# Query tiles of 128, 128, 128, 96 and 96 rows in a decay attention with a routed expert

## The chip, the cores and the metric

One core of a Trainium2 chip runs the whole program. The metric is device time in microseconds (us) of one execution. Engines are named as in the profile: PE multiplies, PEld loads PE's weights beside it, DVE, ACT and POOL do elementwise work, and SP, ACT and POOL issue transfers.

## What is computed

There are 8 batches of 8 heads, 576 tokens and 64 features in a head. Attention is causal, with a bias that decays with a running sum, and is followed by an expert that treats 128 chosen tokens of each batch.

```
scores = scale * q @ k.T;  cum = cumsum(max(s, 0))
scores = where(causal, -1e9, scores + min(-(cum_i - cum_j), 0))
attn = softmax(scores);  x = attn @ v          # heads side by side, 512 wide
score = x @ w_gate;  top = the 128 best tokens of each batch
out = x;  out[top] += sigmoid(score[top]) * (relu(x[top] @ w1) @ w2)
```

## The kernel before

576 tokens are cut into 5 tiles: four of 128 rows and a last one of 64 (`NT = 5`, `LAST = 64`). A head goes through these stages, each an entry of a hand-written list (`SCHEDULE`) that gives a stage its place in a period of 8 slots. Every engine runs its instructions in the order in which the program issues them, since all calls go through `InOrder`, whose line, L34, is the one that the profile shows.

- `s_part` (4 parts): scores with queries on the partitions, only for the row maximum. PE writes `s`, DVE reads it with the mask (`mj`) and leaves the maximum `m`. `m_rows` turns `m` on PE and sends it by ACT and a transfer into row `RM` of `QA`.
- `st_part` (L381, 4 parts): scores again, transposed, with key tile `t` on the partitions and the queries from that tile on along the columns, in two products each (`ka` by `qa`, `kb` by `qb`). Part 0 takes key tiles 1 (448 columns) and 4 (64 keys by 64 queries), part 1 tiles 2 and 3, parts 2 and 3 the two halves of tile 0. ACT takes the exponential into `pt`, and POOL clears the triangle of each tile's own block.
- `av` (L418): for query tile `u`, the sum over key tiles `t <= u` of `pt[t, u]` times `v`; `pt` is the weight operand, so its columns are the query rows. The operands are full-precision f32, and each product runs as two passes. Stage `av0` has tiles 0 and 1, `av1` tile 2, `av2` tile 3, `av3` tile 4. Full tiles take 95 columns of `vt`, the last tile 65 (`VO`, `VC`).
- `norm` (L436): DVE divides by the row sums, and after each 4 heads SP writes the block to `out`, in one transfer for the four full tiles and one for the last.
- `choose` (L482) and `expert` run between these stages in small steps, with `choose` mostly on DVE and `expert` on PE.

Buffers of `s`, `st` and `sct` share 4 PSUM banks (`psS`), so PE can be at most four of them ahead of their readers.

Of the kernel before, what the change touches and what calls it, by code (L numbers as in the profile page):

```python
# [7 lines left out]
F32 = mybir.dt.float32  # L8
F32R = mybir.dt.float32r
# [3 lines left out]
AF = mybir.ActivationFunctionType  # L13
# [6 lines left out]
def _f(ap):  # L20
    return ap.bitcast(F32)
# [45 lines left out]
def kernel(  # L67
# [32 lines left out]
    EPACE, CPACE = CFG["epace"], CFG["cpace"]  # L100


    cols = [S - P * t for t in range(NT)]
    order = [1, 4, 2, 3, 0]
    off = {}
    o = 0
    for t in order:
# [18 lines left out]


    NB = 4
    ka_all = const.tile([P, NB, S], F32R, tag="ka", name="ka")
    kb_all = const.tile([P, NB, S], F32R, tag="kb", name="kb")  # L130
    qa_all = const.tile([P, NB, SP], F32R, tag="qa", name="qa")
    qb_all = const.tile([P, NB, SP], F32R, tag="qb", name="qb")
    KA, KB, QA, QB = ([x[:, i, :] for i in range(NB)] for x in (ka_all, kb_all, qa_all, qb_all))
    warm = const.tile([P, 512], BF16, tag="warm", name="warm")
    dve.memset(warm, 0.0)
    zrow = moe.tile([2 * NH, S], F32, tag="row", name="zrow")
# [36 lines left out]
    act.activation(  # L173
        qa_all[D:RT, 1:NB], warm[D:RT, 0 : NB - 1].rearrange("p (a o) -> p a o", o=1).broadcast_to([RT - D, NB - 1, SP]), AF.Copy, bias=1.0
    )
    pool.memset(_f(ka_all[D:RT, 1:NB]), 1.0)
    maskf, ident = masks()
    pool.memset(_f(qa_all[0:D, :, 0:PAD]), 0.0)

# [28 lines left out]
    def choice_constants():  # L208

        pool.memset(earlier, 1.0)  # L210
        own = earlier[:, (NT - 1) * P : NT * P]
        pool.affine_select(
            out=own, in_=own, pattern=[[-1, P]], compare_op=ALU.is_ge,
            fill=0.0, base=-1, channel_multiplier=1,
        )
        pool.memset(later, 1.0)
        pool.affine_select(
            out=later[:, 0:P], in_=later[:, 0:P], pattern=[[1, P]], compare_op=ALU.is_ge,
            fill=0.0, base=0, channel_multiplier=-1,
        )  # L220
        place_i = moe.tile([P, S], I32, tag="hh", name="place_i")
        pool.iota(place_i, pattern=[[1, S]], base=0, channel_multiplier=0)
        token_i = const.tile([P, NT], I32, tag="token_i", name="token_i")
        pool.iota(token_i, pattern=[[P, NT]], base=0, channel_multiplier=1)
        dve.tensor_copy(place, place_i)
        dve.tensor_copy(token, token_i)
        wgrow = w_gate.rearrange("(o d) -> o d", o=1)
        sp.dma_start(wg, wgrow.broadcast_to([P, DM]))
# [33 lines left out]
    for i in range(2):  # L262
        bank = psA.tile([P, 512], F32, tag=f"av{i}", name=f"pa{i}")
        pa = bank[:, 0 : NT * EW].rearrange("p (t e) -> p t e", e=EW)
        dve.memset(pa[LAST:P, NT - 1, :], 1.0)
        PA.append(pa)


# [112 lines left out]
    def st_part(n, part):  # L381
        i = n % NB
        R = RM[i] + 1
        ka, kb, qa, qb = KA[i], KB[i], QA[i], QB[i]
        if part == 0:
            st[n]["pt"] = ptp.tile([P, PTW], F32, tag="pt", name=f"pt{n}")
        pt = st[n]["pt"]
        tp = psS.tile([P, 512], F32, tag="s", name=f"st{n}_{part}")
        plan = [
            [(1, 0, cols[1]), (4, 0, cols[4])],  # L390
            [(2, 0, cols[2]), (3, 0, cols[3])],
            [(0, 0, HALF)],
            [(0, HALF, HALF)],
        ][part]
        o = 0
        for t, c0, w in plan:
            kr = min(P, S - t * P)
            ks = slice(t * P, t * P + kr)
            qs = slice(PAD + t * P + c0, PAD + t * P + c0 + w)
            pe.matmul(tp[0:kr, o : o + w], ka[0:R, ks], qa[0:R, qs], start=True, stop=False)  # L400
            pe.matmul(tp[0:kr, o : o + w], kb[:, ks], qb[:, qs], start=False, stop=True)
            o += w
        p0 = off[plan[0][0]] + plan[0][1]
        if part == 0:
            act.activation(pt[:, p0 : p0 + cols[1]], tp[:, 0 : cols[1]], AF.Exp, scale=SCALE)
            act.activation(pt[0:LAST, p0 + cols[1] : p0 + o], tp[0:LAST, cols[1] : o], AF.Exp, scale=SCALE)
        else:
            act.activation(pt[:, p0 : p0 + o], tp[:, 0:o], AF.Exp, scale=SCALE)
        for t, c0, _ in plan:
            if c0 == 0:  # L410
                w = min(P, cols[t])
                pool.affine_select(
                    out=pt[0:w, off[t] : off[t] + w], in_=pt[0:w, off[t] : off[t] + w],
                    pattern=[[1, w]], compare_op=ALU.is_ge, fill=0.0, base=0,
                    channel_multiplier=-1,
                )

    def av(n, us):  # L418
        b, h = divmod(n, H)
        pt, vt, pa = st[n]["pt"], vts[n // 2], PA[n % 2]  # L420
        if us[0] == 0:
            if h == 0:
                xts[b] = xp.tile([P, NT, DM], F32, tag="xt", name=f"xt{b}")
        xt = xts[b]
        for u in us:
            w = P if u < NT - 1 else LAST
            for t in range(u + 1):
                kr = P if t < NT - 1 else LAST
                c0 = off[t] + (u - t) * P
                vo, vc, vw = (0, VC[n % 2], EW) if w == P else (VO[n % 2], (n % 2) * E1, E1)  # L430
                pe.matmul(
                    pa[0:w, u, vo : vo + vw], pt[0:kr, c0 : c0 + w], vt[0:kr, t, vc : vc + vw],
                    start=(t == 0), stop=(t == u),
                )

    def norm(n, part):  # L436
        b, h = divmod(n, H)
        xt = xts[b]
        if part == 0:
            st[n]["z"] = small.tile([P, NT], F32, tag="z", name=f"z{n}")  # L440
        z, pa, vo = st[n]["z"], PA[n % 2], VO[n % 2]
        if part == 0:
            dve.tensor_scalar(z, pa[:, :, vo + D], 1e-9, None, op0=ALU.add)
        elif part == 1:
            dve.reciprocal(z, z)
        else:
            dve.tensor_tensor(
                xt[:, :, h * D : (h + 1) * D], pa[:, :, vo : vo + D],
                z.rearrange("p (t o) -> p t o", o=1).broadcast_to([P, NT, D]),
                op=ALU.mult,  # L450
            )
        if part < 2:
            return
        if h % XH == XH - 1:
            es = slice((h + 1 - XH) * D, (h + 1) * D)
            sp.dma_start(
                out[b, 0 : (NT - 1) * P, es].rearrange("(t p) d -> p t d", p=P), xt[:, 0 : NT - 1, es]
            )
            sp.dma_start(out[b, (NT - 1) * P : S, es], xt[0:LAST, NT - 1, es])


    out_rows = out.rearrange("b s d -> (b s) d")
# [19 lines left out]
    def choose(b):  # L482
# [8 lines left out]
                yield CPACE[0]  # L491
        yield CPACE[0]

        row = moe.tile([P, NT * P], F32, tag="row", name=f"row{b}")
        for u0, u1 in ((0, 3), (3, NT)):
            tps = psS.tile([P, 512], F32, tag="s", name=f"sct{b}_{u0}")
            for t in range(u0, u1):
                pe.transpose(
                    tps[:, (t - u0) * P : (t - u0 + 1) * P], sc[:, t : t + 1].broadcast_to([P, P]), ident
                )  # L500
            act.activation(row[:, u0 * P : u1 * P], tps[:, 0 : (u1 - u0) * P], AF.Copy)
            if not finishing:
                yield CPACE[1]
        if finishing:
# [1 line left out]

        ahead = small.tile([P, 2, NT], F32, tag="ahead", name=f"ahead{b}")
        for t in range(NT):
            r = min(P, S - t * P)
            sj = sc[0:r, t : t + 1]  # L510
            for i, (c0, c1, mask, op) in enumerate((
                (0, t * P + r, earlier[0:r, (NT - 1 - t) * P : (NT - 1) * P + r], ALU.is_ge),
                (t * P, S, later[0:r, 0 : S - t * P], ALU.is_gt),
            )):
                junk = moe.tile([P, S], BF16, tag="junk", bufs=2, name=f"ahead{b}_{t}_{i}")
                dve.scalar_tensor_tensor(
                    junk[0:r, 0 : c1 - c0], row[0:r, c0:c1], sj, mask, op0=op, op1=ALU.mult,
                    accum_out=ahead[0:r, i, t : t + 1],
                )
                if not finishing:  # L520
                    yield CPACE[2]

        hits = []
        for si, (s0, n) in enumerate(slots):
            for t in range(NT):
                r = min(P, S - t * P)
                hit = moe.tile([P, P], F16, tag="hit", name=f"hit{b}_{si}_{t}", bufs=NT * len(slots))
                (pool if finishing and t in CFG["hp"] else dve).tensor_scalar(
                    hit[0:r, 0:n], place[0:r, s0 : s0 + n], ahead[0:r, 0, t : t + 1],
                    ahead[0:r, 1, t : t + 1], op0=ALU.subtract, op1=ALU.is_equal,  # L530
                )
                hits.append((hit, si, n, t, r))
                if not finishing:
                    yield CPACE[3]
# [288 lines left out]
```

## Time and profile before

| | us |
|---|---|
| median of 3 runs (lowest, highest) | 543.26 (538.83, 587.77) |
| the profiled execution | 537.0 |
| its span, first to last instruction | 535.2 |
| PE busy in it | 510.6 |
| DVE busy in it | 403.1 |
| POOL busy in it | 324.0 |
| ACT busy in it | 296.6 |

Busy shares are means over stages with different limits, and a PE that is busy is not a PE at its peak: its records overlap. The starts of successive weight loads show better how fast PE gets on.

### The profile page before, as it was taken

The numbers are of one execution on the slowest core, as the hardware profiler recorded it, in microseconds if no ns is written. First come the engines' busy times: TensorE is split into PE (matmuls) and PEld (weight loads), VectorE is DVE, ScalarE is ACT, GpSimd is POOL, SyncE is SP. The second block draws the span as 40 slices with busy tenths as digits, with TensorE's granted clock in tenths as the row PEclk, the third lists the DMA queues.
The fourth block names the chain that finished last, engine by engine and source line by source line (L and its number), as shares of the span: only waits on it lengthen the run. The fifth ranks groups of instructions, "written<-read, shape, count | busy, mean of one in ns | idle before, by whom it ended". The sixth has DMA issues, their size and how long they took to land.

```text
span 535.2 us, 11357 instructions
## 1 busy us (share of the span) xinstructions
PE 510.6 (95%) x3845; PEld 455.7 (85%) x3847; DVE 403.1 (75%) x1416; ACT 296.6 (55%) x658; POOL 324.0 (61%) x492
## 2 busy tenths in 40 slices
PE   6999998999989999999999999999999999999996
PEld 3788988889878888899888999998988898988774
DVE  7668896998899868867768886875689887763642
ACT  5557775657666747555444665544566665532121
POOL 7767775768787767755455774545578764523130
PEclk7999997999999979899999999999999999999999
DMA  4324541243425313323113332033242431011110
GB/s 160 106 97 133 170 142 44 72 141 115 150 75 152 117 59 123 104 89 94 46 69 116 111 114 71 3 116 110 74 132 65 140 95 41 9 46 40 65 39 21
DMA packets 23900, 49.08 MB, mean 92 GB/s; under 512 B 2538, under 2 KB 12069, under 8 KB 23843
## 3 DMA queue, kind: packets, MB, share of 16 engines
q1 hardware_dynamic: 19376, 39.52, 23.2%
q10 hardware_dynamic: 3186, 4.65, 2.8%
q0 software_dynamic: 1280, 4.20, 2.3%
q8 instruction: 30, 0.49, 0.4%
q14 instruction: 28, 0.22, 0.1%
HBM read 36.37 MB, written 11.53 MB: 90 GB/s over the span
## 4 chain that ended last, share of the span: by engine, by line
PE 65%; DVE 23%; issue 6%; DMA 2%; POOL 1%; ACT 1%; POOLq 0%; SPq 0%; DVEq 0%; ACTq 0%
PE pa L34 25%; PE st L34 15%; PE s L34 9%; DVE mj L34 8%; PE py L34 6%; DVE ahead L34 4%; DVE junk L34 3%; DVE qb L34 3%; PE warm L34 2%; DVE xt L34 1%; PE sct L34 1%; POOL hit L34 1%; DMA xe<-out_dram,idx 1%; DVE z L34 1%; DMA out_dram<-xt 1%
## 5 line engine op out<-in xcount | busy, mean ns | idle before, releaser
L34 PE MATMUL pa<-vt,pt 128*128 128x95 f32 (+2 forms) x1920 | 234.1, 261 | 0.0
L34 PEld LDWEIGHTS pa<-vt,pt 128*128 128x128 f32 (+2 forms) x1920 | 215.0, 176 | 18.4 <-issue 10.6
L34 DVE CUSTOM_DVE_ANT_0 mj<-s,maskf 128x192 bf16<-128x192 f32 (+4 forms) x320 | 140.7, 470 | 58.1 <-PE s L34 56.8
L34 ACT ACTIVATE pt<-st 128x288 f32<-128x288 f32 (+3 forms) x320 | 120.3, 430 | 106.4 <-PE st L34 87.6
L34 POOL TENSOR_SCALAR_AFFINE_SELECT pt<-pt 128x128 f32<-128x128 f32 (+1 forms) x320 | 96.1, 321 | 123.6 <-ACT pt L34 111.2
L34 PE MATMUL st<-qa,ka 67*128 67x288 f32 (+9 forms) x384 | 120.2, 330 | 13.5 <-DVE m L34 9.4
L34 POOL TENSOR_TENSOR qb<-qk,qb 64x576 fp32r<-64x576 f32 x62 | 95.7, 1544 | 31.6 <-DVE qb L34 22.1
L34 PE MATMUL s<-ka,qa 66*128 66x64 f32 (+4 forms) x384 | 110.7, 346 | 2.9 <-DVE ka L34 2.9
L34 POOL TENSOR_TENSOR kb<-qk,ka 64x576 fp32r<-64x576 f32 x64 | 95.2, 1488 | 8.2 <-ACT ka L34 3.1
L34 PE MATMUL st<-qb,kb 128*128 128x288 f32 (+4 forms) x384 | 100.1, 298 | 0.0
L34 PEld LDWEIGHTS st<-qa,ka 67*128 67x128 f32 (+3 forms) x384 | 70.6, 184 | 19.4 <-DVE m L34 11.3
L34 PEld LDWEIGHTS st<-qb,kb 128*128 128x128 f32 (+1 forms) x384 | 70.8, 184 | 4.8
L34 PEld LDWEIGHTS s<-ka,qa 66*128 66x128 f32 x384 | 65.4, 194 | 9.6 <-POOL qa L34 3.3
L34 ACT ACTIVATE kb<-qk 64x576 fp32r<-64x576 f32 x64 | 43.6, 683 | 5.4 <-DVE qb L34 1.2
L34 DVE CAST qb<-qk 64x576 fp32r<-64x576 f32 x64 | 44.3, 692 | 2.2 <-issue 0.2
L34 ACT ACTIVATE qa<-qk 64x576 fp32r<-64x576 f32 x64 | 43.7, 683 | 3.4 <-DMA qa<-mr 1.5
L34 ACT ACTIVATE ka<-qk 64x576 fp32r<-64x576 f32 x64 | 42.9, 670 | 4.1 <-DVE m L34 3.6
L34 ACT ACTIVATE mr<-s 5x128 fp32r<-5x128 f32 x63 | 16.8, 266 | 47.8 <-PE s L34 47.4
L34 DVE CUSTOM_DVE_ANT_0 junk<-xt,wg 128x512 bf16<-128x512 f32 (+1 forms) x40 | 37.4, 954 | 0.4
L34 DVE TENSOR_TENSOR xt<-pa,z 128x320 f32<-128x320 f32 x64 | 31.1, 486 | 0.1
L34 DVE SCALAR_TENSOR_TENSOR ahead<-row,sc,later 128x576 bf16<-128x576 f32 (+4 forms) x35 | 29.4, 840 | 0.6
L34 POOL DMA_INDIRECT out_dram<-xe,idx x8 | 8.5, 1068 | 33.6 <-DVE xe L34 24.2
(284 smaller groups left out, 534.5 us busy)
## 6 DMA issues: line engine op xcount, KB each, us to landing
qk<-in_qk_dram SPq DMA_DIRECT2D x31, 576.0 KB
vt<-in_v_dram SPq DMA_DIRECT2D x32, 325.0 KB
out_dram<-xt SPq DMA_DIRECT2D x16, 512.0 KB
wr<-in_w_dram ACTq DMA_DIRECT2D x16, 256.0 KB
out_dram<-xt SPq DMA_DIRECT2D x16, 64.0 KB
ka<-cumhl ACTq DMA_DIRECT2D x63, 4.5 KB
qa<-mr ACTq DMA_DIRECT2D x63, 2.5 KB
qk<-in_qk_dram SPq DMA_DIRECT2D x2, 288.0 KB
```

Source lines behind the costliest of these rows:

```text
L34: return self._tc.keep_in_program_order(call(*args, **kwargs))
```

## The change

The 576 query rows are cut into 128, 128, 128, 96 and 96. Key tiles stay 128 wide, but the last one, of 64 keys, is filled to 96 with zero columns in `ka` and `kb`. Query tile 4 begins at row 480 and key tile 4 at 512, so the triangle that POOL clears in it is shifted (`base`), and clears the added keys as well. The block of key tile 4 is now 96 by 96, and moves from part 0 of `st_part` to part 3. In `av` every product writes 95 columns; tiles 3 and 4 have 96 weight columns. The output of 576 rows is written as 384 and 192 rows. `choose` follows the new tiles. `s_part` and `m_rows` stay as they are.

```diff
-    cols = [S - P * t for t in range(NT)]
-    order = [1, 4, 2, 3, 0]
+    NF = NT - 2
+    R1 = (S - NF * P) // 2
+    QR = [P] * NF + [R1, R1]
+    QB0 = [min(P * u, NF * P) + max(0, u - NF) * R1 for u in range(NT)]
+    KR = [P] * (NT - 1) + [R1]
+    SK = (NT - 1) * P + R1
+    cols = [S - x for x in QB0]
+    order = [1, 2, 3, 0, 4]
...
+    pool.memset(_f(ka_all[:, :, S:SK]), 0.0)
+    pool.memset(_f(kb_all[:, :, S:SK]), 0.0)
...
+        pool.iota(token_i[:, NT - 1 : NT], pattern=[[P, 1]], base=QB0[NT - 1], channel_multiplier=1)
...
         plan = [
-            [(1, 0, cols[1]), (4, 0, cols[4])],
+            [(1, 0, cols[1])],
             [(2, 0, cols[2]), (3, 0, cols[3])],
             [(0, 0, HALF)],
-            [(0, HALF, HALF)],
+            [(0, HALF, HALF), (4, 0, cols[4])],
         ][part]
...
         for u in us:
-            w = P if u < NT - 1 else LAST
+            w = QR[u]
+            vc = VC[n % 2]
             for t in range(u + 1):
-                kr = P if t < NT - 1 else LAST
-                c0 = off[t] + (u - t) * P
-                vo, vc, vw = (0, VC[n % 2], EW) if w == P else (VO[n % 2], (n % 2) * E1, E1)
+                c0 = off[t] + QB0[u] - QB0[t]
                 pe.matmul(
-                    pa[0:w, u, vo : vo + vw], pt[0:kr, c0 : c0 + w], vt[0:kr, t, vc : vc + vw],
+                    pa[0:w, u, :], pt[0 : KR[t], c0 : c0 + w], vt[0 : KR[t], t, vc : vc + EW],
                     start=(t == 0), stop=(t == u),
                 )
...
-            sp.dma_start(
-                out[b, 0 : (NT - 1) * P, es].rearrange("(t p) d -> p t d", p=P), xt[:, 0 : NT - 1, es]
-            )
-            sp.dma_start(out[b, (NT - 1) * P : S, es], xt[0:LAST, NT - 1, es])
+            sp.dma_start(out[b, 0 : NF * P, es].rearrange("(t p) d -> p t d", p=P), xt[:, 0:NF, es])
+            sp.dma_start(out[b, NF * P : S, es].rearrange("(t p) d -> p t d", p=R1), xt[0:R1, NF:NT, es])
```

## Rows read from the trace of the kernel before

**Rows 1.** Part 1 of the page: busy us, share of the span, instructions.

```profile
PE 510.6 (95%) x3845; PEld 455.7 (85%) x3847; DVE 403.1 (75%) x1416; ACT 296.6 (55%) x658; POOL 324.0 (61%) x492
```

**Rows 2.** Waits, of the whole span: engine and tile that waited, for whom; us in total, times, longest us.

```profile
PEld pa L34 <- issue: 10.6, 63, 0.4
PE st L34 <- DVE m L34: 9.4, 13, 1.4
```

**Rows 3.** Timeline of one head without side work, 299.8 to 306.2 us, weight loads and one piece of products: start us, us, engine, instruction, count, and in brackets idle time before it.

```profile
300.74 0.14 PEld L34 LDWEIGHTS st<-qb,kb 128*64 128x64 f32 x1
...
300.91 0.19 PEld L34 LDWEIGHTS st<-qb,kb 128*128 128x128 f32 x1
...
301.31 0.75 PEld L34 LDWEIGHTS pa<-vt,pt 128*128 128x128 f32 x6
...
301.98 0.19 PEld L34 LDWEIGHTS s<-ka,qa 66*128 66x128 f32 x1
...
302.88 0.19 PEld L34 LDWEIGHTS s<-ka,qa 66*128 66x128 f32 x1
...
303.88 0.41 ACT L34 ACTIVATE pt<-st 128x288 f32<-128x288 f32 x1
...
304.42 0.30 PEld L34 LDWEIGHTS s<-ka,qa 66*128 66x128 f32 x2
...
304.88 0.80 PEld L34 LDWEIGHTS pa<-vt,pt 128*64 128x64 f32 x10 [0.16 <-issue]
...
304.98 0.40 POOL L34 TENSOR_SCALAR_AFFINE_SELECT pt<-pt 128x128 f32<-128x128 f32 x1
...
305.74 0.30 PEld L34 LDWEIGHTS s<-ka,qa 66*128 66x128 f32 x2
...
305.11 0.45 PE L34 MATMUL pa<-vt,pt 128*64 128x65 f32 x5
```

**Rows 4.** Groups by form, whole span: engine, operation, weight rows*columns, shapes, count, busy us, mean ns of one, idle us before them.

```profile
L34 PEld LDWEIGHTS pa<-vt,pt 128*128 128x128 f32 x1280 | 168.4, 196 | 3.4 <-POOL pt L34 0.4
L34 PEld LDWEIGHTS pa<-vt,pt 128*64 128x64 f32 x512 | 34.6, 137 | 10.7 <-issue 10.6
L34 POOL TENSOR_SCALAR_AFFINE_SELECT pt<-pt 64x64 f32<-64x64 f32 x64 | 16.8, 263 | 0.0
L34 ACT ACTIVATE pt<-st 64x64 f32<-64x64 f32 x64 | 13.1, 205 | 0.0
L34 PEld LDWEIGHTS s<-ident,m 128*5 128x5 f32 x63 | 5.3, 85 | 1.1
```

**Rows 5.** Busy time of each engine by stretch: us from the span's start, length, then PE, PEld, DVE, ACT and POOL busy us (instructions), granted clock, share and GB/s of the transfers. Each stretch begins at the first 192-column score product of a head; in order they hold heads 3 to 11, 12 and 13, 15 to 17, 20 and 21, 23 to 25, 28 to 32, 41, 44, 45 to 52, 53, 55 to 57, and 60, counted from 1.

```profile
19.37:72.60 53.23, 52.48 (x408) 46.14 (x411) 40.19 (x148) 37.67 (x84) 40.02 (x67) 1.00 0.41 129
72.60:89.69 17.09, 15.64 (x103) 14.47 (x103) 13.88 (x45) 10.39 (x24) 11.84 (x17) 0.80 0.38 120
...
96.02:115.79 19.77, 18.47 (x154) 16.84 (x154) 19.48 (x71) 12.83 (x29) 14.71 (x23) 1.00 0.25 81
...
127.57:140.90 13.33, 12.44 (x104) 11.34 (x103) 12.48 (x43) 8.64 (x20) 10.67 (x17) 1.00 0.48 156
...
147.23:169.96 22.73, 19.34 (x154) 17.17 (x153) 22.47 (x72) 14.07 (x31) 18.86 (x26) 1.00 0.32 99
...
182.02:220.62 38.60, 35.99 (x257) 33.11 (x256) 31.78 (x110) 23.29 (x52) 28.62 (x40) 0.87 0.37 115
...
291.46:298.55 7.09, 6.52 (x56) 5.88 (x56) 6.99 (x26) 4.64 (x11) 5.20 (x9) 1.00 0.14 50
...
310.73:318.56 7.83, 7.83 (x68) 7.39 (x67) 7.68 (x26) 4.50 (x10) 5.12 (x9) 1.00 0.61 184
318.56:388.31 69.75, 69.21 (x537) 63.40 (x535) 48.27 (x181) 36.59 (x85) 37.32 (x58) 1.00 0.23 74
388.31:395.79 7.48, 6.57 (x55) 5.91 (x54) 6.93 (x25) 4.58 (x11) 6.40 (x10) 1.00 0.33 100
...
401.88:421.74 19.86, 18.61 (x155) 16.91 (x154) 19.58 (x71) 12.87 (x29) 15.01 (x23) 1.00 0.25 78
...
433.92:441.74 7.82, 7.82 (x68) 7.39 (x67) 7.67 (x26) 4.50 (x10) 5.11 (x9) 1.00 0.57 169
```

**Rows 6.** Timeline of PE at three of its waits: start us, us, instruction, idle time before it and what ended it.

```profile
82.54 0.61 PE L34 MATMUL st<-qa,ka 67*128 67x320 f32 x1 [1.34 <-DVE m L34]
...
214.89 0.41 PE L34 MATMUL st<-qa,ka 67*128 67x320 f32 x1 [1.44 <-DVE m L34]
...
394.60 0.40 PE L34 MATMUL st<-qa,ka 67*128 67x288 f32 x1 [0.91 <-DVE md L34]
```

**Rows 7.** Stretches of 3.4 to 6.9 us at and after those waits, in the columns of rows 5.

```profile
82.59:89.42 6.83, 6.83 (x31) 6.73 (x31) 4.09 (x14) 3.47 (x7) 3.53 (x8) 0.50 0.00 0
...
215.71:219.12 3.41, 3.41 (x18) 3.23 (x16) 3.00 (x10) 1.55 (x3) 3.33 (x6) 0.50 0.67 190
...
391.00:397.90 6.90, 5.99 (x50) 5.40 (x50) 5.71 (x27) 4.45 (x10) 5.83 (x8) 1.00 0.02 6
```

**Rows 8.** Timeline of POOL and PE in the first 9 us.

```profile
6.49 0.20 POOL L34 MEMSET ident<- 128x128 f32 x1
...
7.10 0.30 POOL L34 MEMSET qa<- 64x256 f32 x1
...
8.26 1.19 PE L34 MATMUL s<-ka,qa 66*128 66x192 f32 x3 [2.86 <-DVE ka L34]
```

More of the change, by code (lines that the diff above doesn't have):

```diff
@@ L128 @@
     NB = 4
-    ka_all = const.tile([P, NB, S], F32R, tag="ka", name="ka")
-    kb_all = const.tile([P, NB, S], F32R, tag="kb", name="kb")
+    ka_all = const.tile([P, NB, SK], F32R, tag="ka", name="ka")
+    kb_all = const.tile([P, NB, SK], F32R, tag="kb", name="kb")
     qa_all = const.tile([P, NB, SP], F32R, tag="qa", name="qa")
     qb_all = const.tile([P, NB, SP], F32R, tag="qb", name="qb")
-    KA, KB, QA, QB = ([x[:, i, :] for i in range(NB)] for x in (ka_all, kb_all, qa_all, qb_all))
+    QA, QB = ([x[:, i, :] for i in range(NB)] for x in (qa_all, qb_all))
+    KA, KB = ([x[:, i, 0:S] for i in range(NB)] for x in (ka_all, kb_all))
     warm = const.tile([P, 512], BF16, tag="warm", name="warm")
@@ L175 @@
     )
-    pool.memset(_f(ka_all[D:RT, 1:NB]), 1.0)
+    pool.memset(_f(ka_all[D:RT, 1:NB, 0:S]), 1.0)
+    pool.memset(_f(ka_all[:, :, S:SK]), 0.0)
+    pool.memset(_f(kb_all[:, :, S:SK]), 0.0)
     maskf, ident = masks()
@@ L264 @@
         pa = bank[:, 0 : NT * EW].rearrange("p (t e) -> p t e", e=EW)
-        dve.memset(pa[LAST:P, NT - 1, :], 1.0)
+        dve.memset(pa[R1:P, NF:NT, :], 1.0)
         PA.append(pa)
@@ L383, in st_part @@
         R = RM[i] + 1
-        ka, kb, qa, qb = KA[i], KB[i], QA[i], QB[i]
+        ka, kb, qa, qb = ka_all[:, i, :], kb_all[:, i, :], QA[i], QB[i]
         if part == 0:
@@ L396, in st_part @@
         for t, c0, w in plan:
-            kr = min(P, S - t * P)
+            kr = KR[t]
             ks = slice(t * P, t * P + kr)
-            qs = slice(PAD + t * P + c0, PAD + t * P + c0 + w)
+            qs = slice(PAD + QB0[t] + c0, PAD + QB0[t] + c0 + w)
             pe.matmul(tp[0:kr, o : o + w], ka[0:R, ks], qa[0:R, qs], start=True, stop=False)
@@ L403, in st_part @@
         p0 = off[plan[0][0]] + plan[0][1]
-        if part == 0:
-            act.activation(pt[:, p0 : p0 + cols[1]], tp[:, 0 : cols[1]], AF.Exp, scale=SCALE)
-            act.activation(pt[0:LAST, p0 + cols[1] : p0 + o], tp[0:LAST, cols[1] : o], AF.Exp, scale=SCALE)
+        if part == 3:
+            act.activation(pt[:, p0 : p0 + HALF], tp[:, 0:HALF], AF.Exp, scale=SCALE)
+            act.activation(pt[0:R1, p0 + HALF : p0 + o], tp[0:R1, HALF:o], AF.Exp, scale=SCALE)
         else:
@@ L410, in st_part @@
             if c0 == 0:
-                w = min(P, cols[t])
+                w = KR[t]
                 pool.affine_select(
                     out=pt[0:w, off[t] : off[t] + w], in_=pt[0:w, off[t] : off[t] + w],
-                    pattern=[[1, w]], compare_op=ALU.is_ge, fill=0.0, base=0,
+                    pattern=[[1, w]], compare_op=ALU.is_ge, fill=0.0, base=QB0[t] - t * P,
                     channel_multiplier=-1,
@@ L492, in choose @@
         yield CPACE[0]
-        row = moe.tile([P, NT * P], F32, tag="row", name=f"row{b}")
+        row = moe.tile([P, S], F32, tag="row", name=f"row{b}")
         for u0, u1 in ((0, 3), (3, NT)):
@@ L497, in choose @@
             for t in range(u0, u1):
+                r, c0 = QR[t], QB0[t] - QB0[u0]
                 pe.transpose(
-                    tps[:, (t - u0) * P : (t - u0 + 1) * P], sc[:, t : t + 1].broadcast_to([P, P]), ident
+                    tps[:, c0 : c0 + r], sc[0:r, t : t + 1].broadcast_to([r, P]), ident[0:r, 0:r]
                 )
-            act.activation(row[:, u0 * P : u1 * P], tps[:, 0 : (u1 - u0) * P], AF.Copy)
+            c0, c1 = QB0[u0], QB0[u1 - 1] + QR[u1 - 1]
+            act.activation(row[:, c0:c1], tps[:, 0 : c1 - c0], AF.Copy)
             if not finishing:
@@ L508, in choose @@
         for t in range(NT):
-            r = min(P, S - t * P)
+            r, q0 = QR[t], QB0[t]
             sj = sc[0:r, t : t + 1]
             for i, (c0, c1, mask, op) in enumerate((
-                (0, t * P + r, earlier[0:r, (NT - 1 - t) * P : (NT - 1) * P + r], ALU.is_ge),
-                (t * P, S, later[0:r, 0 : S - t * P], ALU.is_gt),
+                (0, q0 + r, earlier[0:r, (NT - 1) * P - q0 : (NT - 1) * P + r], ALU.is_ge),
+                (q0, S, later[0:r, 0 : S - q0], ALU.is_gt),
             )):
@@ L525, in choose @@
             for t in range(NT):
-                r = min(P, S - t * P)
+                r = QR[t]
                 hit = moe.tile([P, P], F16, tag="hit", name=f"hit{b}_{si}_{t}", bufs=NT * len(slots))
```

## The prediction

> **What bounds the kernel now.** I read the busy shares first. PE is busy 95% of the span and its weight loads 85%, DVE 75%, POOL 61% and ACT 55% [rows 1]: PE is the first suspect, DVE the second. The waits bear this out: PE's products of `st` waited 9.4 us in all for DVE's maxima, in 13 pieces [rows 2], so nearly everywhere else PE ran from one instruction into the next. The stretches then split the 64 heads in two kinds. In heads 3 to 11 and 45 to 52 DVE is busy 76% and 69% of the time and PE and its loads fill it [rows 5]: there a shorter PE shortens the stretch. In heads 15 to 17, 20, 21, 23 to 25, 41, 44, 53, 55 to 57 and 60 DVE is busy 93% to 99% [rows 5], with the steps of `choose` on top of its row maxima: there PE waits for DVE already, or would as soon as it is faster. The heads that rows 5 leave out are of the first kind.
>
> What PE does in a head is read from the starts of weight loads, since a product can't start before its load. Six loads of 128 columns from 301.31 to the next load at 301.98 are 0.112 us each; the half-size products start 0.057 us apart (0.45 less one of about 0.22, over 4) [rows 3]. The passes of `av` go at the pace of their weight columns. A 512-column score product with six full passes takes 0.90 (301.98 to 302.88) [rows 3]: 0.34 for the scores, and 5 x 0.112, the sixth load being hidden behind the scores. Two score products of 192 and 320 columns have one more load boundary, about 0.03, so 0.37. With the half-size group behind them I expect 0.37 + 9 x 0.057 = 0.88. It takes 1.32 (304.42 to 305.74) [rows 3]. The missing 0.44 is neither load nor product. Part of it is visible as idle time of the loader with nothing that it waits for, 0.16 here, 63 times and 10.6 us in the span [rows 2, 3]; the rest lies inside the group of ten, which lasts 0.86 instead of 0.57 [rows 3].
>
> **The change part by part.**
>
> `av3`, query tile 4: its ten passes go from 64 to 96 weight columns. No row has 96 columns. The duration of a load is 85 ns for 5 columns, 137 for 64 and 196 for 128 [rows 4], nearly a straight line, so I take the pace between 0.057 and 0.112, which is 0.085 us (bounds: those two). If the gaps go away: 0.37 + 9 x 0.085 = 1.135 instead of 1.32, a gain of 0.185 us.
>
> `av2`, query tile 3: its eight passes go from 128 to 96 columns, 8 x (0.112 - 0.085) = 0.215 us gained. The contraction over 96 instead of 64 keys adds no instruction.
>
> `st_part`: the two products with key tile 4 go from 64 to 96 columns, and move from part 0 to part 3. Before, they cost 0.17 us, from 300.74 to 300.91 [rows 3], which is one load of 64 and one of 128. After: 0.085 + 0.112 = 0.197, so 0.03 lost.
>
> One rule of the notes speaks against the change. The Trainium skill, "TensorE: Matmul & The Clock Gate", section "LDWEIGHTS (loading the stationary operand)", has the load time grow with the columns alone. A head now loads 3264 columns in `av` instead of 3200, and 64 more in `st`: by that rule alone the change costs 128 columns, some 0.1 us in a head. The trace agrees on the columns and contradicts the sum, since 0.44 us of the half-size group are not loads.
>
> Another rule explains the 0.44. "TensorEngine Tiling (Array Packing)", section "Key Properties", also of the Trainium skill, says that a change of tiling mode drains the engine. By it the 64-column products of `st` would drain too, and at a third of the 0.44 for each of three changes, the two around `st` would bring 0.29 us more in a head, 13 us over the 45 heads that count below. The row denies that for them: 0.17 us is loads alone, so I price nothing there.
>
> Sum for PE: 0.185 + 0.215 - 0.03 = 0.37 us in a head. Between the bounds of a 96-column pass the sum runs from a gain of 0.9 (pace 0.057) to a loss: at 0.112, `av2` gains nothing, `av3` loses 0.06 and `st` 0.05.
>
> Edits costed at nothing. The two new memsets on POOL at the start are 128 x 128 elements each; `ident`'s of that size took 0.20. They push `qa`'s memset from its end at 7.40 to about 7.8, and PE's first score product waits until 8.26 for DVE [rows 8]; without that cover they cost 0.4. ACT's exponential of 64 x 64 (0.205 us) becomes 96 x 96, below the 0.41 of a 288-column one, so at most 0.2 more; POOL's triangle (0.263) grows less than 0.1 [rows 3, 4]. Both engines are far from full [rows 1]. The moved triangle waits on POOL for ACT's last exponential, with `qlo` of a later head behind it; but ACT starts the fourth part's exponential at 303.88 and would be through by 304.6, and POOL comes to tile 0's triangle only at 304.98 [rows 3]. `av3`, which needs it, is ten slots later. The output has the same bytes in 32 transfers as before, with 384 and 192 rows; `norm`, DVE's maxima and `m_rows` are untouched, and `choose` has as many instructions on DVE.
>
> What of 64 x 0.37 arrives? In the 15 heads with DVE at 93% or more [rows 5] nothing: what PE saves becomes a longer wait of `st` for `m`. Heads 12, 13 and 28 to 32 have both kinds; their long waits of 1.34 and 1.44 [rows 6] show DVE late, and I count 3 of the 7. That leaves 45 heads, 45 x 0.37 = 16.7 us. The profiled execution took 537.0, so its like would take 520.3. The two lower runs shown are 1.8 and 6.3 us above the profiled one, and I add 3: 523 us against the median of 543.26.
>
> **The rivals.**
>
> A. The longer waits cost clock. After the waits of 1.34 and 1.44 us the granted clock fell to 0.50, that is 1.2 GHz, for 6.83 and 3.41 us, after that of 0.91 it stayed at 1.00 [rows 6, 7]. In a stretch of 6.83 us at half clock PE got through 31 products, which at the pace of head 53 (55 in 6.57 [rows 5]) take 3.7, so 3.1 are lost. The change lengthens waits in DVE-bound heads by up to 0.37: 0.91 becomes 1.28. For it: ten or so such waits are left, of 0.6 on the mean [rows 2, 6]. Against it: the idle time moves from inside the half-size group to the wait, and the products of the head get wider rather than fewer. With one to four new falls the time is 526 to 536; I put the rival at 530 to 537, with three or four.
>
> B. DVE gives way: its row maxima start earlier because PE writes scores earlier, and all 64 heads gain: 23.7 us, 513 to 516. Against it: 98% or 99% busy leaves no room in 23 to 25, 15 to 17 and 55 to 57 [rows 5].
>
> C. The change doesn't remove the gaps: the 0.44 belong to something else at that place in the program, or a 96-column load goes at the pace of 128. Then `av3` loses 9 x 0.028 = 0.25 against 0.215 - 0.03 gained: 0.07 in a head, 3 us, or, by the loads, 0.11, 5 us: 540 to 545 with the same 3 added. For it: the trace names no cause ("issue") [rows 2]; against it: the gaps stand only at the 64-column f32 passes, while 1280 loads of 128 columns have 3.4 us of idle time before them in all [rows 4].
>
> D, the other side: a 96-wide group is itself a smaller form and pays on entry and exit. Then both `av2` and `av3` have gaps of x, against one of 0.44 now: 2x - 0.44 + 0.07 more in a head. With x = 0.44 that is 0.51, some 23 us, 563. It makes the kernel slower by over 2% from x = 0.31 on (0.24 x 45 = 10.9). Against it: products of other widths, 5 columns of `m` among them, show 1.1 us of idle time before 63 loads [rows 4].
>
> **How the numbers follow.** Forecast 52%, 517 to 529, at 523; A 20%; B 12%; C 10%; D 6%. The range of 512 to 537 takes in forecast, A and B; what is left out is C and D, and little of the rest. About 2%, 10.9 us, is what a measurement of this kernel can tell from no change, so faster means below 532.4. Faster: nearly all of the forecast, all of B and a fifth of A, 65%. Same: most of A, C, and the upper end of the forecast, 30%. Slower: D, 5%.
>
> **What would show it.** In the profile of the changed kernel loads of `pa` with 96 columns should last about 165 ns and follow each other at 0.085 us; the loader's idle time put down to "issue" before `pa` (10.6 us) should be gone; two score products and `av3` should take 1.14 instead of 1.32, with `av2` 0.2 shorter. In DVE-bound heads the stretch keeps its length and PE's waits for `m` grow, to some 15 us in all. Gaps before 96-column loads would mean D, the same gaps at `av3` alone C, further stretches at clock 0.50 A. If DVE-bound stretches shrink too, B is right. The forecast is wrong above all if the pace of a 96-column pass is not 0.085.

## The result and the profile after

The changed kernel takes 521.47 us (median of 4 runs, 518.85 to 522.36). Measured beside it, the kernel before had a median of 558.41 (4 runs, 538.83 to 587.77); the ratio is 0.963, with an interval of 0.954 to 0.972. The runs of the kernel before lie in two groups, at 534 to 551 and at 557 to 595 us, the second with PE's clock low for longer; the ratio leaves that group out, and those of the experiments leave out every run of this kernel above 542 us.

The profiled execution took 521.3 us with a span of 519.6, against 537.0 and 535.2. Busy time, in the columns of [rows 1]:

```profile
PE 487.6 (94%) x3845; PEld 447.5 (86%) x3847; DVE 401.9 (77%) x1416; ACT 302.8 (58%) x658; POOL 332.5 (64%) x495
```

PE has as many instructions as before and 23 us less busy time. The weight loads by form answer to [rows 4]: 167 ns for 96 columns, and no idle time put down to "issue" any more.

```profile
L34 PEld LDWEIGHTS pa<-vt,pt 128*96 128x96 f32 x1024 | 102.8, 167 | 0.7
...
L34 PEld LDWEIGHTS pa<-vt,pt 96*96 96x96 f32 x128 | 16.0, 164 | 0.0
```

The loads of one head answer to [rows 3]: start, us, instruction, count.

```profile
414.10 0.16 PEld L34 LDWEIGHTS st<-qa,ka 67*96 67x96 f32 x1
414.23 0.16 PEld L34 LDWEIGHTS st<-qb,kb 128*96 128x96 f32 x1
414.31 0.76 PEld L34 LDWEIGHTS pa<-vt,pt 128*96 128x96 f32 x8
414.99 0.30 PEld L34 LDWEIGHTS s<-ka,qa 66*128 66x128 f32 x2
415.22 0.99 PEld L34 LDWEIGHTS pa<-vt,pt 128*96 128x96 f32 x10
416.13 0.19 PEld L34 LDWEIGHTS s<-ka,qa 66*128 66x128 f32 x1
```

Eight loads of `av2` take 0.68 us, 0.085 each. Two score products and `av3` take 1.14 (414.99 to 416.13) instead of 1.32. The pair of `st` loads costs 0.21.

Stretches, in the columns of [rows 5]: heads 3 to 11, 15 to 17, 23 to 25, 44, 45 to 52, 53, 55 to 57 and 60, then two at low clock, which answer to [rows 7].

```profile
20.56:72.47 51.91, 50.53 (x411) 45.50 (x411) 40.36 (x148) 38.24 (x85) 41.01 (x67) 1.00 0.43 132
...
93.90:113.89 19.99, 17.82 (x156) 16.45 (x154) 19.67 (x75) 13.31 (x29) 15.54 (x24) 1.00 0.26 78
...
147.26:170.09 22.83, 18.70 (x155) 16.61 (x154) 22.53 (x76) 14.41 (x32) 19.95 (x27) 1.00 0.33 98
...
302.23:309.68 7.45, 7.45 (x69) 7.36 (x67) 7.32 (x25) 4.77 (x11) 5.40 (x9) 1.00 0.63 182
309.68:376.78 67.10, 66.17 (x537) 62.94 (x535) 47.82 (x181) 37.11 (x84) 38.22 (x59) 1.00 0.23 76
376.78:383.88 7.10, 6.08 (x56) 5.64 (x54) 6.76 (x25) 4.67 (x11) 6.47 (x9) 1.00 0.41 122
389.61:409.51 19.90, 17.83 (x156) 16.43 (x154) 19.64 (x71) 13.29 (x29) 16.04 (x24) 1.00 0.25 78
420.94:428.38 7.44, 7.44 (x69) 7.35 (x67) 7.31 (x25) 4.76 (x11) 5.41 (x9) 1.00 0.57 162
83.93:87.34 3.41, 3.41 (x19) 3.41 (x19) 3.29 (x8) 2.03 (x5) 2.40 (x4) 0.50 0.00 0
135.13:141.95 6.82, 6.82 (x36) 6.72 (x36) 2.90 (x11) 3.66 (x8) 4.19 (x6) 0.50 0.29 81
```

The three stretches of three heads under a full DVE are as long as before (19.77, 22.73 and 19.86 us in [rows 5]). Heads 45 to 52 are 2.65 us shorter, heads 3 to 11 only 1.32. Heads 44, 53 and 60 got 0.38 shorter each, though DVE was as full there (98%, 93% and 98% before). What PE saved in the three long stretches became waiting, in the columns of [rows 2]:

```profile
PE st L34 <- DVE m L34: 17.0, 22, 1.7
```

In heads 3 to 11 the weight loader waits for DVE's `m` as well, which takes back about half of what PE saved there. The lines show the loader's waits in these heads, first of the kernel before (19.37 to 72.60 us) and then of the changed one (20.56 to 72.47); the four waits stand in heads 5, 7, 9 and 11, which got no shorter.

```profile
PEld st L34 <- DVE m L34: 0.4, 1, 0.4
```

```profile
PEld st L34 <- DVE m L34: 2.2, 4, 0.9
```

The start got worse. Instructions of DVE, POOL and PE there, in order of time, first of the kernel before and then of the changed one:

```profile
7.03 0.24 DVE L34 MEMSET pa<- 64x95 f32 x2
7.30 0.81 DVE L34 SCALAR_TENSOR_TENSOR ka<-cumh,odd,cum 2x576 fp32r<-2x576 f32 x1
7.48 1.90 POOL L34 TENSOR_TENSOR kb<-qk,ka 64x576 fp32r<-64x576 f32 x1
```

```profile
7.06 0.42 DVE L34 MEMSET pa<- 32x190 f32 x2
...
7.49 1.40 POOL L34 TENSOR_TENSOR kb<-qk,ka 64x576 fp32r<-64x576 f32 x1
7.51 1.99 DVE L34 SCALAR_TENSOR_TENSOR ka<-cumh,odd,cum 2x576 fp32r<-2x576 f32 x1
...
9.65 1.19 PE L34 MATMUL s<-ka,qa 66*128 66x192 f32 x3 [3.60 <-DVE ka L34]
```

PE's first score product waits for DVE's write of `ka`, and starts at 9.65 instead of 8.26.

### The profile page after: what moved, and what is told of

Same layout as the page of the kernel before. It is cut to its first block, busy times and chain, and to the rows that moved or that the text cites. A ratio compares the mean times of both kernels' runs of the same rounds, so it can differ in the third digit from the quotient of the medians.

```text
span 519.6 us, 11361 instructions
## 1 busy us (share of the span) xinstructions
PE 487.6 (94%) x3845; PEld 447.5 (86%) x3847; DVE 401.9 (77%) x1416; ACT 302.8 (58%) x658; POOL 332.5 (64%) x495
## 4 chain that ended last, share of the span: by engine, by line
PE 58%; DVE 27%; issue 8%; DMA 3%; ACT 2%; POOL 1%; ACTq 0%; POOLq 0%; SPq 0%; DVEq 0%
PE pa L34 22%; PE st L34 14%; DVE mj L34 10%; PE s L34 7%; PE py L34 6%; DVE ahead L34 4%; DVE qb L34 3%; DVE junk L34 3%; PE warm L34 2%; DVE xt L34 1%; DMA out_dram<-xt 1%; DVE z L34 1%; ACT pt L34 1%; PE sct L34 1%; POOL hit L34 1%
## 5 line engine op out<-in xcount | busy, mean ns | idle before, releaser
L34 PE MATMUL pa<-vt,pt 128*96 128x95 f32 (+2 forms) x1920 | 227.4, 260 | 0.0
L34 PEld LDWEIGHTS pa<-vt,pt 128*96 128x96 f32 (+2 forms) x1920 | 214.7, 177 | 3.7 <-POOL pt L34 0.4
L34 ACT ACTIVATE pt<-st 128x288 f32<-128x288 f32 (+3 forms) x320 | 128.4, 439 | 105.2 <-PE st L34 88.5
L34 POOL TENSOR_SCALAR_AFFINE_SELECT pt<-pt 128x128 f32<-128x128 f32 (+1 forms) x320 | 108.1, 356 | 107.4 <-ACT pt L34 99.4
L34 PE MATMUL s<-ka,qa 66*128 66x64 f32 (+4 forms) x384 | 109.1, 342 | 3.6 <-DVE ka L34 3.6
L34 POOL TENSOR_TENSOR qb<-qk,qb 64x576 fp32r<-64x576 f32 x62 | 92.6, 1494 | 23.9 <-DVE qb L34 15.0
L34 PE MATMUL st<-qb,kb 128*128 128x288 f32 (+4 forms) x384 | 102.0, 302 | 0.0
L34 PEld LDWEIGHTS st<-qa,ka 67*128 67x128 f32 (+3 forms) x384 | 71.9, 187 | 32.5 <-DVE m L34 27.1
L34 PEld LDWEIGHTS st<-qb,kb 128*128 128x128 f32 (+1 forms) x384 | 72.3, 188 | 0.8
L34 DVE CUSTOM_DVE_ANT_0 junk<-xt,wg 128x512 bf16<-128x512 f32 (+1 forms) x40 | 34.9, 892 | 0.4
```

The costliest lines, as they stand in the source:

```text
L34: return self._tc.keep_in_program_order(call(*args, **kwargs))
```

## Experiments

A plain head, from its first score product to the next head's, is the cleanest measure of PE's pace. This is the mean of heads 18, 42 and 58, as far as each runs at a granted clock of 1.00 (e4: without 18).

| kernel | plain head, us | runs, us | ratio to the kernel before |
|---|---|---|---|
| before | 5.90 | 534 to 595 | |
| changed | 5.51 | 519 to 524 | 0.963 (0.954 to 0.972); as f4, 0.976 (0.970 to 0.981) |
| e1, tile 3 loads 128 | 5.73 | 523 to 535 | 0.982 (0.970 to 0.993) |
| e2, tile 4 loads 64 | 5.81 | 533 to 537 | 0.999 (0.994 to 1.004) |
| e3, 64 keys | 5.85 | 533 to 542 | 1.002 (0.990 to 1.013) |
| e4, v 65 wide in both tiles | 5.52 | 570 to 582 | 1.071 (1.061 to 1.082) |
| f1, before with v 95 wide | 6.14 | 545 to 627 | none |
| f2, v 65 wide in tile 4 | 5.52 | 520 to 546 | 0.984 (0.971 to 0.998) |

**e1: tile 3 back to 128 columns.**

```diff
-            w = QR[u]
+            w = P if u == NF else QR[u]
```

> The changed kernel, but query tile 3 loads 128 weight columns in av again (32 rows are computed twice, nothing is left out). My account: the pace of a pass is its weight load, 0.112 us at 128 columns and 0.085 at 96, so av2 costs 8 x 0.027 = 0.215 us more in a head, over the 45 heads that PE limits 9.7 us: about 531 where the changed kernel takes 521. Rival (the narrower tile 3 brings nothing, all of the gain is the missing gaps): 521.

Measured: 529.81 us, and 0.215 us more in a plain head (5.73 against 5.51). The eight loads of `av2` take 0.89 us instead of 0.68:

```profile
305.03 0.97 PEld L34 LDWEIGHTS pa<-vt,pt 128*128 128x128 f32 x8
305.92 0.30 PEld L34 LDWEIGHTS s<-ka,qa 66*128 66x128 f32 x2
```

The narrower tile 3 is worth what its loads cost, which is over half of the change's 0.39 in a head. The total is a weaker witness: the runs go from 523 to 535 us, and the profiled one (534.75) has 23.9 us at half clock (1.2 GHz), around a wait of 2.65 us for DVE (to 83.58):

```profile
82.74:106.63 23.89, 23.05 (x105) 22.54 (x106) 12.24 (x52) 9.28 (x20) 8.61 (x14) 0.50 0.12 40
```

**e2: tile 4 with 64 weight columns.**

```diff
-        dve.memset(pa[R1:P, NF:NT, :], 1.0)
+        dve.memset(pa[LAST:P, NF:NT, :], 1.0)
...
-            w = QR[u]
+            w = LAST if u == NT - 1 else QR[u]
```

> The changed kernel, but query tile 4 loads only its first 64 weight columns in av; its last 32 rows are left out. The contraction stays at 96 or 128 keys. My account: weights of 64 columns or fewer in f32 products change the form of the array, one entry and one exit per head at a third of 0.44 us each; ten loads at 0.057 instead of 0.085 nearly pay for them: 0.29 - 0.25 = 0.04 us in a head, 2 us, so about 523, with the loader's idle time before pa (issue) back at some 10 us. Rival (the gaps came from the contraction over 64 keys): no gaps, and 0.25 us less in a head, about 510.

Measured: 535.26 us, and 0.29 more in a plain head instead of 0.04. The idle time is back:

```profile
L34 PEld LDWEIGHTS pa<-vt,pt 128*64 128x64 f32 x512 | 44.1, 137 | 10.8 <-issue 10.7
```

So weights of 64 columns alone bring the gaps, as my account has it. Its size was off because I took the passes at 0.057; that was the pace with 65 columns of `v`, and here they have 95 (f1 gives the pace).

**e3: the last product over 64 keys.**

```diff
-  pt[0 : KR[t], ...], vt[0 : KR[t], ...]
+  pt[0:kr, ...], vt[0:kr, ...]      # kr = 64 for the last key tile
```

> The changed kernel, but the last product of av3 contracts over the 64 real keys instead of 96 rows with zeros; weights stay 96 columns wide. My account: a contraction over 64 rows is another form too, one entry and one exit in a head, some 0.29 us, 13 us over 45 heads: about 534. Rival (only the width of the weights counts): 521, no idle time of the loader before pa.

Measured: 538.2 us, 0.33 more in a plain head. Two score products and `av3` take 1.47 us (302.96 to 304.43) instead of 1.14:

```profile
302.96 0.30 PEld L34 LDWEIGHTS s<-ka,qa 66*128 66x128 f32 x2
303.18 1.16 PEld L34 LDWEIGHTS pa<-vt,pt 128*96 128x96 f32 x10
304.43 0.30 PEld L34 LDWEIGHTS s<-ka,qa 66*128 66x128 f32 x2
```

Here the loads are as wide as in the changed kernel, and only two passes contract over 64 rows. Half the rows costs about as much as half the columns; both had to go.

**e4: 65 columns of v in the 96-row tiles.**

```diff
-  pa[0:w, u, :], ..., vt[0 : KR[t], t, vc : vc + EW]
+  pa[0:w, u, vo : vo + vw], ..., vt[0 : KR[t], t, vc : vc + vw]    # vw = 65 where w < 128
```

> The changed kernel, but the two 96-row tiles write 65 columns of v instead of 95 (nothing of the result is left out). My account: the pass goes at the pace of its 96-column load, 0.085 us, whatever the product's width: 521, same pace. Rival (the product of 95 f32 columns sets the pace): passes of 0.06 to 0.08 us, 18 of them in a head, 4 to 20 us less.

Measured: 575.42 us, with a plain head of 5.52 us at full clock. The load does set the pace, and yet the kernel is 10% slower than the changed one. The granted clock shows why (columns of [rows 5]):

```profile
83.90:189.70 105.80, 105.80 (x510) 103.31 (x509) 52.00 (x207) 46.48 (x99) 47.60 (x76) 0.50 0.20 64
189.70:227.30 37.60, 34.71 (x296) 32.31 (x296) 35.43 (x127) 25.80 (x57) 29.39 (x42) 1.00 0.47 143
227.30:261.40 34.10, 34.10 (x164) 33.24 (x163) 18.20 (x68) 15.11 (x33) 18.71 (x26) 0.50 0.24 74
```

After a wait of 1.78 us for DVE the clock fell to half, 1.2 GHz, and stayed there for 106 us, in which PE waited for nothing; later for another 34. I had no theory for this.

**e5: DVE relieved, in both kernels.**

```diff
+  if b == 0: score(b, sc, t, DM)        # batches 1 to 6: no scores, no ranking
...
+  ahead = aheads[b if first else 0]     # batch 0's ranks
```

> The kernel before with DVE relieved: batches 1 to 6 leave out the scores by w_gate, their turning and the ranking, and take batch 0's ranks instead (other tokens are chosen). All slots and all work of the expert stay. My account: PE's waits for m and the falls of the clock that follow them go, so some 15 us less than the kernel before. It is the base for the next run.

> The changed kernel with the same relief of DVE and the same parts left out. My account: with DVE no longer the limit anywhere, all 64 heads gain 0.37 us, so it is about 23 us faster than the kernel before with the relief (16 to 17 without it). Rival (the heads with a full DVE were not held by DVE, or the gain is not one of PE's pace in each head): the difference stays at 16.

Measured: the changed kernel with the relief takes 497.00 us (496.61 to 498.03); the kernel before with it ran from 525.01 to 611.45, and its profile was at half clock from 82.5 to 242.9 us. So I compare heads 33 to 63, at clock 1.00 in all four profiles; first the pair with the relief (before, then changed), then the pair without:

```profile
273.03:515.05 242.02, 241.40 (x1933) 223.33 (x1933) 151.21 (x576) 136.49 (x312) 140.13 (x228) 1.00 0.26 85
```

```profile
200.69:430.63 229.94, 229.55 (x1934) 222.26 (x1933) 149.73 (x576) 140.32 (x314) 142.78 (x230) 1.00 0.29 90
```

```profile
220.62:469.17 248.55, 244.73 (x1954) 225.74 (x1953) 190.80 (x688) 140.06 (x320) 146.80 (x225) 1.00 0.25 81
```

```profile
215.17:455.17 240.00, 233.84 (x1954) 223.58 (x1953) 190.21 (x692) 143.63 (x321) 152.52 (x228) 1.00 0.27 86
```

The change gains 12.1 us in these 31 heads with DVE relieved (0.39 each, all of them), and 8.6 without. DVE withholds the rest. The total of the first run expected here came out otherwise: the relief did not rid the kernel before of low clock.

**e6: the memsets of pa later.**

```diff
-        dve.memset(pa[R1:P, NF:NT, :], 1.0)        # while the banks are set up
+        for pa in PA: dve.memset(pa[R1:P, NF:NT, :], 1.0)   # after ("qb", 0)
```

> The changed kernel, but DVE's two memsets of pa are issued after the first heads' first steps instead of before the split of the running sums. My account of the late start (first score product at 9.65 us instead of 8.26): these memsets grew from 0.24 to 0.42 us, so that DVE's split of the sums no longer starts ahead of POOL's subtraction for kb but just behind it, and takes 1.99 us instead of 0.81. Without them the product starts at about 8.2 us and the whole kernel is 1.4 us faster. Rival (the two new memsets on POOL make the start late): it stays at 9.6.

Measured: the time is 519.90 us (517.73 to 520.95). The split of the sums starts at 7.03 and takes 0.81 again, and the first score product starts at 7.99:

```profile
7.03 0.81 DVE L34 SCALAR_TENSOR_TENSOR ka<-cumh,odd,cum 2x576 fp32r<-2x576 f32 x1
...
7.99 0.73 PE L34 MATMUL s<-ka,qa 66*128 66x192 f32 x4 [1.53 <-DVE ka L34]
```

The start is shown; the gain in the total, 1.5 us against the changed kernel, is near the spread.

**e7: qb on ACT in all heads.**

```diff
-        dve.tensor_copy(QB[n % NB][D:P, PAD:SP], st[n]["q"])
+        act.activation(QB[n % NB][D:P, PAD:SP], st[n]["q"], AF.Copy)
```

> The changed kernel, with the copy qb (0.70 us in a head) on ACT instead of DVE. My account: in the some 19 heads where DVE is the limit each gets up to 0.37 us shorter, and waits of PE shrink: 5 to 7 us less, about 515. Rival (ACT, at 64% to 84% in heads, becomes late with its exponentials, and the move only shifts the wait): 521 or more.

Measured: 535.32 us. The rival holds: full DVE stretches shrink (head 56 from 6.76 to 5.97 us), but other heads now wait up to 2.5 us, and `av` waits for POOL's triangles behind late exponentials:

```profile
PE pa L34 <- POOL pt L34: 8.3, 4, 2.5
```

A part of the loss is clock: this profile has 20.5 us at half clock, the changed kernel's 10.2.

**f1 to f4: width and clock, and a faster version.** f1 gives the last tile of the kernel before 95 columns of `v`; f2 gives only tile 4 of the changed kernel 65.

```diff
f1
-  vo, vc, vw = (0, VC[n % 2], EW) if w == P else (VO[n % 2], (n % 2) * E1, E1)
+  vo, vc, vw = 0, VC[n % 2], EW
```

> The kernel before, but its last tile of 64 rows writes 95 columns of v like the others (nothing is left out). The passes go at 0.081 instead of 0.057 (the pace seen for 64 weight columns with 95 columns of v), so each head that PE limits is 0.24 us longer and an execution at full clock takes about 548. Theory that the width of the products brings the clock back: stretches at half clock stay below some 25 us, and no run is above 560, while the kernel before has runs at 570 and more. Rival (the half-size form or the waits keep the clock down, the width does not matter): runs at 570 and more here too, as often as before.

> The changed kernel, but tile 4 alone writes 65 columns of v; tile 3 keeps 95. Loads and their pace are as in the changed kernel, so at full clock 521. Theory (the width of the products): some of the runs have long stretches at half clock, as the kernel before, 540 to 570. Rival (it takes all 18 narrow passes, or it was chance): 518 to 523 in all runs.

f1 measured: a plain head of 6.14, 0.24 more, as expected for ten passes at 0.081; but 575.13 us in the median, with 44 and 17 us at half clock:

```profile
173.60:218.00 44.40, 44.40 (x194) 40.19 (x195) 20.86 (x78) 18.04 (x39) 17.74 (x29) 0.50 0.22 69
218.00:235.00 17.00, 15.74 (x127) 14.08 (x126) 14.02 (x49) 11.72 (x27) 12.14 (x17) 1.00 0.33 107
235.00:252.00 17.00, 17.00 (x75) 15.77 (x76) 11.08 (x38) 6.76 (x14) 8.68 (x14) 0.50 0.22 70
```

So the width alone does not bring the clock back where the gaps remain. f2 measured: 527.99 us, 519.66 to 546.0 where the changed kernel stays within 520 to 524; ten narrow passes already cost clock in some runs.

```diff
f3, with e6
+  if n > 8 and n % H in (6, 7, 0): act.activation(QB[...], q, AF.Copy)
+  else: dve.tensor_copy(QB[...], q)
```

> The changed kernel with both the later memsets of pa and the copy qb on ACT, but qb only for the heads 6, 7 and 0 of a period of 8 from head 14 on, in which DVE is the limit. My account: ACT is at 60% to 67% there and has room, so the two gains add without the waits for ACT and POOL that the move in all heads brought: 1.6 for the start and 3 to 6 for DVE, 513 to 517. Rival (any copy moved makes ACT late): 520 or more.

> The changed kernel itself, unaltered, as the base for the other three on the same chip: 518 to 523 in all runs by every theory.

f3 measured: 512.07 us (509.88 to 516.74), f4 521.37 (519.72 to 524.13) beside it, so f3 is the fastest kernel here: 0.958 of the kernel before (0.949 to 0.968) where f4 is at 0.976 (0.970 to 0.981). Heads 55 to 57 take 18.27 us instead of 19.90:

```profile
382.57:400.84 18.27, 17.62 (x155) 16.43 (x154) 18.12 (x68) 14.76 (x33) 15.30 (x24) 1.00 0.28 86
```

## Why the prediction was right, and where it was wrong

**PE's pace: right, and shown.** The pace of a 96-column pass is 0.085, the two score products with `av3` fell to 1.14, `av2` by 0.21. Predicted 0.37 in a head, measured 0.39 (5.90 to 5.51). e1 and e2 hold its two halves apart. By the same runs C and D fall: the "issue" gaps are gone and no new ones stand at 96 columns.

**Only heads with room on DVE gain: right in the main, but DVE's share was the wrong test.** The three long stretches under a full DVE did not shorten, and e5 shows that DVE is the reason. But of the 15 heads put at nothing, 44, 53 and 60 gained 0.38 each. In 44 and 60 PE was busy without a break (7.83 of 7.83 and 7.82 of 7.82 us in [rows 5]), so a DVE at 98% had not held it up. The other way round, heads 3 to 11, with DVE at 76% and counted among the 45, gave 1.32 us of 3.3: in four of them the loader now waits for `m`, 2.2 us in all. Of 15.6 us less span, about 3.1 are less time at half clock (10.2 us instead of 17.1, at the 3.1 lost in 6.83 of the prediction's A), and the late start took back 1.4; so pace brought 13.9, not 16.7. At the measured 0.39 that is 36 heads' worth instead of 45. B falls with the three long stretches. That 521.3 came out where the prediction added up 520.3 is in part luck: less from pace, the late start and the time won at half clock nearly cancel.

**An edit costed at nothing: wrong.** I named POOL's two memsets, which cost nothing (`qa`'s memset starts at 7.10 in both kernels, not 0.4 later), and left out that DVE's memsets of `pa` become wider. They are 0.18 us longer, and DVE's next instruction then starts just behind POOL's subtraction for `kb` (7.49) instead of ahead of it, and takes 1.99 instead of 0.81. e6 shows it. POOL's triangle grew by 0.13 us (0.391 against 0.263), more than the 0.1 put down for it; nothing shows that it cost time.

**The clock and the level: the step that failed.** "The two lower runs shown are 1.8 and 6.3 us above the profiled one, and I add 3" took it that the changed kernel's runs scatter as the kernel before's do, and set the sum against a median of 543.26; A let the clock enter only as a loss. The term of 3 measured 0.2: the changed kernel's runs lie from 518.85 to 522.36, with the median of 521.47 beside a profiled 521.3. The kernel before went to 587.77 in the same measurement, and its median to 558.41, 21 us above its profiled execution. So the gain between the medians is 37 us, not 20. The ratio of 0.963 is the 3.7% that was forecast, but it rests on two runs of the kernel before (538.83 and 543.26); beside f4, against runs of that kernel at 534 to 536, it is 0.976, and from profile to profile the span fell by 2.9%.

A's premise held only in part. Waits did grow to 17.0 us, and both falls of the changed kernel's clock came behind long ones (1.66 us, to 82.22, and 1.16, to 134.01). But two more, of 1.25 and 1.16 us (to 150.65 and 190.86), were followed by a clock of 1.00, and there were two stretches at half clock instead of three. The third of the kernel before, which [rows 7] does not have, came behind a wait of 1.07 us; its line is the first here, the two others are the changed kernel's.

```profile
191.82:198.65 6.83, 6.83 (x31) 6.73 (x31) 3.30 (x13) 3.12 (x8) 3.52 (x8) 0.50 0.00 2
```

```profile
134.01 0.41 PE L34 MATMUL st<-qa,ka 67*128 67x320 f32 x1 [1.16 <-DVE m L34]
```

```profile
150.65 0.41 PE L34 MATMUL st<-qa,ka 97*128 97x320 f32 x1 [1.25 <-DVE m L34]
```

What the change does for the clock was shown only in part. Narrow passes without gaps (e4) and wide passes with gaps (f1) both leave PE at half clock for 44 to 106 us; the changed kernel has neither, and its longest such stretch was 6.8 us. But e1 has neither and stayed there for 23.9 us, and e2 and e3 have gaps and wide passes, and no run above 542. Which of the remaining differences decides stays open.

## What to carry to other kernels

A tail tile that halves a dimension can cost more than its columns save: compare what a group takes with what its loads and products take, and split the last two tiles evenly instead. Price a saving on the limiting engine head by head, since it only arrives where the next engine has room, and a little work moved off that engine in just those heads (f3) beats moving it everywhere (e7). Before trusting a median, look at how far its runs scatter and at the granted clock of the profile.

## What the runs showed of the hardware

A pass costs the longer of its load and its product, as far as these widths show it: 96 weight columns with 65 or 95 columns of `v` both go at 0.085 us (e4, changed), 64 weight columns at 0.057 with 65 columns (before) and, from f1's 0.24 us in ten passes, at 0.081 with 95. The gaps belong to f32 products whose weights are 64 columns wide or whose contraction is 64 rows; each costs about 0.3 us per group (e2, e3). "TensorEngine Tiling (Array Packing)" of the Trainium skill, section "Key Properties", says that a change of tiling mode drains the engine. That these products are such a change is my reading of it: the gaps of e2 and e3 agree, and the 64-column products of `st` in [rows 3] don't show one. Once the granted clock has fallen, a PE that waits for nothing can stay at half for 106 us (e4). An instruction of POOL can lengthen one of DVE: the same DVE instruction of 576 elements took 0.81 us where it started ahead of POOL's subtraction (kernel before, e6), and 1.99 where it started 0.02 us behind it (changed kernel).
